# Block-sparse attention with an exact-GELU feed-forward layer: the queries' transposition moved next to the keys', and the scale of 1/8 moved from the queries to the keys

## The chip, the cores and the metric

The kernel runs on one core of one Trainium2 chip. A core has five engines that run on their own and wait for each other by semaphores: TensorE (PE in the profile, with its weight loads as PEld), VectorE (DVE), ScalarE (ACT), GpSimd (POOL) and SyncE (SP). SyncE and GpSimd also issue transfers, each through a queue of its own that is worked off in order. The metric is the device time of one execution in microseconds, as a median of several runs. Before the change it is 324.17 us (three runs, 323.64 to 324.26). One more execution was recorded by the hardware profiler; all times of single instructions come from it.

## What is computed

Four batches, eight heads, 768 tokens, 64 numbers a head. The tokens form 24 blocks of 32. A block of queries sees its neighbours, the first and the last block and three sampled blocks; the first and the last block of queries see everything. The attention's output, 3072 tokens of 512 numbers, goes through a feed-forward layer with GELU:

```python
scores = (1.0 / np.sqrt(D)) * np.matmul(q, k.transpose(0, 1, 3, 2))
mask = np.abs(blk_i - blk_j) <= 1
mask = mask | (blk_i == 0) | (blk_j == 0) | (blk_i == n_blocks - 1) | (blk_j == n_blocks - 1)
# ... and the three sampled key blocks of each query block
attn = softmax(np.where(mask, scores, -1e9))
x = np.matmul(attn, v)            # heads side by side: 3072 x 512
h = x @ w_in                      # 512 -> 2048
out = (0.5 * h * (1.0 + erf(h / np.sqrt(2)))) @ w_out   # 2048 -> 512
```

With D = 64 the scale of the scores is 1/8, a power of two. It may stand on the queries or on the keys: in bf16 both give the same scores.

## The kernel before, in words

The work is cut into nine units. Batch 0 has three (units 0, 1 and 2, of one, two and three groups of 128 tokens), each further batch two halves of three groups. The first half of a batch also holds its dense rounds, those of the first and the last query block (4 rounds); the other rounds take two query blocks each. A second half has six rounds.

The main loop over units `n` (from L574) does this for each: VectorE gathers the sampled keys and values of the next unit into `gb` (L269), FFN1 of unit n runs in eight steps (L451, with GELU on ScalarE in L454), and then comes the attention of unit n + 1, with pieces of FFN2 of unit n between its rounds as filler for PE (L470). In a round (`attention`, L495) PE makes scores of queries `qT` against keys (L305), VectorE takes maxima (L330, or L333 for a dense round), ScalarE takes exponentials (L342), VectorE turns the probabilities (L359; L363 into `ptd` for a dense round), and PE weighs the values (L405, L381). The iteration `it` of that loop issues the scores of round it + 1 and the exponentials of round it; a dictionary of hooks adds work at a chosen `it`, behind the stores that are ready (`store_finished`) and ahead of the filler.

A new batch needs its keys and queries with the head dimension on partitions. For batch 0 PE turns them at the start and ScalarE copies them out (`place_heads`). For the later batches GpSimd loads keys (`kn`) and then queries (`qn`) by token, twelve transfers (L111), during FFN1 of the last unit but one of the batch before. Two transfers on SyncE's queue then turn them:

- `turn_keys` (L117) writes `ptd`. It is hooked in at it = 4 of the second half's attention, while `ptd` is not in use.
- `turn_queries` (L120) writes `qT`, of which there are two buffers by batch. It is issued behind the first step of FFN1 of the second half, where `n` is the last unit of its batch (`fresh`).

At that place VectorE then works off, in order: `place_keys` (L123, from `ptd` into `kv`), a spare key block (L240), the fixed part of the gathers (L253, L258, L260), the 33 sampled gathers (L269) and `scale_queries` (L128), which multiplies all of `qT` by 1/8 in place. In the same step GpSimd starts eight loads of values (`load_v`, L134) for the batch that follows the next one, as long as there is one: so in FFN1 of the second halves of batches 0 and 1, and not in that of batch 2.

SyncE's queue otherwise carries the stores of the output (L461). Their tiles (`os`) have three buffers. In the second half of batch 0 a store falls behind round it = 1; in the second halves of batches 1 and 2 one falls behind it = 0 and one behind it = 3.

Of the kernel before, what the change touches and what calls it, by code (L numbers as in the profile page):

```python
# [19 lines left out]
def kernel(  # L20
# [10 lines left out]
    nc = tc.nc  # L31
    P = 128
    B, H, S, D = q.shape
    assert (B, H, S, D) == (4, 8, 768, 64)
    BL = 32
    NB = S // BL
# [4 lines left out]
    NPR = H // 2  # L41
# [6 lines left out]
    PI = 8  # L48
# [6 lines left out]
    NC = S // P  # L55
# [17 lines left out]
    qT0 = const.tile([P, NC, NPR, P], BF16, name="qT0")  # L73
    qT1 = const.tile([P, (NB + 1) * KC], BF16, name="qT1")
    qTs = [qT0, qT1[:, 0:NPR * S].rearrange("p (c r s) -> p c r s", r=NPR, s=P)]
    k0 = qT1.rearrange("p (n c) -> p n c", c=KC)
# [21 lines left out]
    def keys(b):  # L98
        return kvs[b % 2][:, :, 0:KC]
# [5 lines left out]
    def by_token(x):  # L105
        return x.rearrange("p h c -> p (h c)")[:, 0:S * H * D // P]
# [6 lines left out]

    kTd = ptd.rearrange("p g c x q e -> p (g c x q e)")

    def turn_keys(b):
        nc.sync.dma_start_transpose(out=kTd.rearrange("p (n s) -> p n s", s=P), in_=by_token(kn))  # L117

    def turn_queries(b):
        nc.sync.dma_start_transpose(out=qTs[b % 2].rearrange("p c r s -> p (c r) s"), in_=by_token(qn))  # L120

    def place_keys(b):
        nc.vector.tensor_copy(  # L123
            keys(b)[:, 0:NB].rearrange("p (c n) (r k) -> p c n r k", c=NC, k=BL),
            kTd.rearrange("p (c r n k) -> p c n r k", c=NC, r=NPR, k=BL))

    def scale_queries(b):
        nc.vector.tensor_scalar_mul(qTs[b % 2], qTs[b % 2], 1.0 / 8.0)  # L128

    def load_v(b, h):  # L130
        G, hh = divmod(h, 4)
        c0 = KC + V2 * G + VW * (hh % 2)
        hh ^= G
        nc.gpsimd.dma_start(out=kvs[b % 2][32 * hh:32 * hh + 32, 0:NB, c0:c0 + D],  # L134
                            in_=v[b, h].rearrange("(n p) d -> p n d", p=BL))
# [13 lines left out]
    def hold_loads(m):  # L149

        nc.gpsimd.tensor_copy(mark, g[0:1, m, 0:1])  # L151
# [52 lines left out]
    def block_numbers(js, engine):  # L204
        flat = vf.rearrange("o j r -> o (j r)")
        vals = []
        for c0 in range(js[0] * NR, (js[-1] + 1) * NR, 22):
            c1 = min(c0 + 22, (js[-1] + 1) * NR)
            _, got = nc.values_load_multi_w_load_instructions(
                flat[0:1, c0:c1], engines=[engine], min_val=0, max_val=NB,  # L210
                skip_runtime_bounds_check_because="block numbers are below the number of blocks")
            vals += got if isinstance(got, (tuple, list)) else [got]
        return {j: vals[NR * i:NR * i + NR] for i, j in enumerate(js)}
# [9 lines left out]

    def place_heads(which, pr, pt):
        if which == "k":
            nc.scalar.copy(k0[:, 0:NB, BL * pr:BL * pr + BL].rearrange("q n (a i) -> q n a i", i=PI),
                           pt.rearrange("q i (n a) -> q n a i", n=NB))
        else:
            nc.scalar.mul(qT0[:, :, pr, :].rearrange("q c (p i) -> q c p i", i=PI),
                          pt.rearrange("q i (c p) -> q c p i", c=NC), 1.0 / 8.0)  # L230

    def spaces():

# [8 lines left out]
    def gather_fixed(kT, place):  # L242

        groups = gb.rearrange("p (g x) -> p g x", x=GW)
        js = sorted(place)
        runs = [[j for j in js if place[j] - j == c] for c in sorted({place[j] - j for j in js})]
        for run in runs:
            i0 = place[run[0]]
            assert i0 % 3 == 0
            for lane in range(min(3, len(run))):  # L250
                m, g0 = len(range(lane, len(run), 3)), i0 // 3
                c0, j = BW + KC * lane, run[0] + lane - 1
                nc.vector.tensor_copy(  # L253
                    groups[:, g0:g0 + m, c0:c0 + 3 * BW].rearrange("p g (w c) -> p g w c", c=BW)[:, :, :, 0:KC],
                    kT[:, j:j + 3 * m, :].rearrange("p (g w) c -> p g w c", w=3))
        at = slice(min(place.values()) // 3, max(place.values()) // 3 + 1)
        n = at.stop - at.start
        nc.vector.tensor_copy(groups[:, at, 0:3 * KC].rearrange("p g (l c) -> p g l c", c=KC),  # L258
                              kT[:, None, 0:1, :].to_broadcast([P, n, 3, KC]))
        nc.vector.tensor_copy(  # L260
            groups[:, at, 4 * BW:GW].rearrange("p g (l x) -> p g l x", x=DW)[:, :, :, NR * BW:DW],
            kT[:, None, NB - 1:NB, :].to_broadcast([P, n, 3, KC]))

    def gather(unit, js, at, c0=0, c1=BW, engine=None):

        src = k0 if (unit.b, c1) == (0, KC) else kvs[unit.b % 2][:, :, c0:c1]
        for j in js:
            for r in range(NR):
                (engine or nc.vector).tensor_copy(sampled(unit.place[j], r)[:, None, c0:c1],  # L269
                                                  src[:, bass.ds(at[j][r], 1), :])  # L270
# [175 lines left out]
    def ffn1_step(n, m):  # L446
        T = P * len(units[n].quads)
        hp = psA.tile([P, 2, 512], F32, name="hp", tag="A")
        for i in range(2):
            for ki in range(KIN):  # L450
                nc.tensor.matmul(hp[:, i, 0:T], lhsT=w_in_sb[:, ki, (m + i) * P:(m + i + 1) * P],  # L451
                                 rhs=xTs[n % 2][:, ki, 0:T], start=(ki == 0), stop=(ki == KIN - 1))
        for i in ((0, 2),) if m < KOUT - 2 else ((0, 1), (1, 2)):
            nc.scalar.activation(g[:, m + i[0]:m + i[1], 0:T], hp[:, i[0]:i[1], 0:T], AF.Gelu)  # L454
# [119 lines left out]
    for n, unit in enumerate(units):  # L574
        nxt = units[n + 1] if n + 1 < len(units) else None
        b = unit.b
        fresh = nxt is not None and nxt.b != b
        if nxt is not None and not fresh:
            gather_fixed(k0 if n == 0 else keys(b), nxt.place)
            if n == 0:  # L580
                known |= block_numbers(J0[:3], DVE)
                gather(nxt, J0[:3], known, 0, KC)
                gather(nxt, J0[:3], known, KC, BW)
            elif n == 1:
                known |= block_numbers(J1[:6], DVE)
                gather(nxt, J1[:6], known)
                gather(nxt, J1[6:7], block_numbers(J1[6:7], DVE))
            else:
                gather(nxt, J1[:6], known)
                for js in (J1[6:9], J1[9:11]):  # L590
                    gather(nxt, js, block_numbers(js, DVE))
        for s in range(KOUT // 2):
            ffn1_step(n, 2 * s)
            if s == 0:
                if n == 0:
                    hold_loads(0)
                    for h in range(H):
                        load_v(1, h)
                    nc.gpsimd.tensor_copy(kvs[0][:, :, 0:KC], k0)
                    gather(units[2], J1[7:], block_numbers(J1[7:], POOL), engine=nc.gpsimd)  # L600
                if n > 0 and not fresh and b + 1 < B:
                    hold_loads(0)
                    load_by_token(kn, k, b + 1)
                    load_by_token(qn, q, b + 1)
                if fresh and b + 2 < B:
                    hold_loads(0)
                    for h in range(H):
                        load_v(b + 2, h)
                if fresh:
                    others = block_numbers(J0[7:], DVE)  # L610
            if s == 7 and nxt is not None:
                table(AF.Exp)
            if fresh and s == 0:
                turn_queries(b + 1)
                place_keys(b + 1)
                spare_key(keys(b + 1))
                gather_fixed(keys(b + 1), nxt.place)
                gather(nxt, J0[:7], known)
                gather(nxt, J0[7:], others)
                scale_queries(b + 1)  # L620
        filler = ffn2_pieces(n)
        if nxt is None:
            last_output(n)
        elif n in QUOTAS:
            attention(nxt, filler, *QUOTAS[n],
                      hooks={4: [lambda: turn_keys(1)]} if n == 1 else None)
        elif fresh:
            attention(nxt, filler, [6, 6, 4, 0, 6, 6, 4, 0, 2, 2, 1], (6, 3), late=True)
        else:
            attention(nxt, filler, [8, 8, 5, 5, 6, 2, 2], (3, 6),  # L630
                      hooks={4: [lambda: turn_keys(b + 1)]} if b + 1 < B else None)


# [28 lines left out]
```

## Time and profile before

| what | us |
|---|---|
| median of three runs | 324.17 |
| the profiled execution's own time | 323.12 |
| its span, first to last instruction | 321.3 |
| PE busy in the span | 262.8 |
| VectorE busy | 220.1 |
| ScalarE busy | 208.7 |
| GpSimd busy | 87.1 |
| one turn of queries, issue to landing (least, median, most) | 5.5, 10.0, 11.3 |
| one turn of keys, issue to landing (least, median, most) | 6.1, 6.4, 7.2 |

A row of the order of time begins with start and length in microseconds, then engine, line, operation and tiles, how many instructions are put together, and in square brackets the idle time of the engine just before them and what ended it. "issue" means that the profile shows nothing for which the engine waited. In the groups of instructions "x3 | 2.9, 961" is three instructions, 2.9 us busy, 961 ns each on average. An "SPq" or a transfer in GpSimd's rows is the time that issuing took; the transfer itself lands later.

### The profile page before, as it was taken

To read this page: it belongs to the slowest core of one execution; us is meant where nothing else is said; L and a number is where in the kernel's file an instruction comes from. 1 tells how busy PE (TensorE), PEld (TensorE's weight loads), DVE (VectorE), ACT (ScalarE), POOL (GpSimd) and SP (SyncE) were. 2 spreads that over 40 slices of the span, in tenths; PEclk is the share of its full clock that TensorE was granted. 3 is DMA by queue.
4 is the path that set the end of the run, shared out by engine and by line. 5 is a ranking of instruction groups with operands and counts; after the bars stand their busy time and mean duration, and the time that the engine had idled before them with its cause. 6 is when DMAs were issued, how large, how long until landed. Compare 5 with 4: busy or idle time off the path is not lost.

```text
span 321.3 us, 12117 instructions
## 1 busy us (share of the span) xinstructions
PE 262.8 (82%) x5240; PEld 147.9 (46%) x5240; DVE 220.1 (68%) x544; ACT 208.7 (65%) x374; POOL 87.1 (27%) x147
## 2 busy tenths in 40 slices
PE   1755864985798867999996887999898889989995
PEld 0614722743453444535552444535453555445543
DVE  6488783787497886868694897768588878583000
ACT  9665483489266794688564785688468876777621
POOL 8569766670070000870070000950000000000000
PEclk9999696699999999999997999999999999999999
DMA  7999999797099110596699010993540100011001
GB/s 111 142 115 207 207 121 26 76 146 142 4 155 73 38 37 4 64 148 114 114 147 46 35 37 37 69 162 86 94 93 33 37 4 35 1 37 37 33 35 66
DMA packets 90632, 25.43 MB, mean 79 GB/s; under 512 B 81745, under 2 KB 87634, under 8 KB 90578
## 3 DMA queue, kind: packets, MB, share of 16 engines
q0 software_dynamic: 68352, 13.64, 84.3%
q1 hardware_dynamic: 22226, 11.01, 13.8%
q8 instruction: 41, 0.67, 0.9%
q14 instruction: 13, 0.11, 0.1%
HBM read 27.26 MB, written 6.29 MB: 104 GB/s over the span
## 4 chain that ended last, share of the span: by engine, by line
PE 45%; DVE 16%; DMA 12%; issue 11%; ACT 9%; POOL 5%; DVEq 0%; SPq 0%; ACTq 0%; POOLq 0%
PE hp L451 19%; PE op L470 12%; DMA qT<-qn 7%; ACT pp L342 7%; PE av L405 5%; DVE nm L330 4%; DVE pT L359 4%; PE sc L305 4%; DVE xh L422 3%; DMA w_in_sb<-in_moe_w_in_dram 3%; DMA kv<-in_v_dram 2%; POOL kn L111 2%; PE av L491 2%; POOL qn L111 2%; PE op L491 2%
## 5 line engine op out<-in xcount | busy, mean ns | idle before, releaser
L342 ACT ACTIVATE pp<-sc,nm 128x256 bf16<-128x256 f32 (+1 forms) x192 | 92.2, 592 | 20.3 <-DVE nm L330 9.9
L451 PE MATMUL hp<-xT,w_in_sb 128*128 128x384 bf16 (+2 forms) x576 | 89.3, 320 | 1.8 <-ACT xT L437 1.6
L470 PE MATMUL op<-w_out_sb,g 128*128 128x512 bf16 x336 | 86.9, 385 | 2.7 <-ACT os L459 2.6
L454 ACT ACTIVATE g<-hp 128x768 bf16<-128x768 f32 (+4 forms) x81 | 53.8, 676 | 38.7 <-PE hp L451 38.6
L451 PEld LDWEIGHTS <-w_in_sb 128*128 128x128 bf16 x576 | 57.0, 104 | 35.1 <-issue 4.1
L330 DVE TENSOR_REDUCE nm<-sc 128x4 f32<-128x1024 f32 (+1 forms) x48 | 53.3, 1111 | 8.4 <-PE sc L305 8.1
L269 DVE COPY gb<-kv 128x388 bf16 (+1 forms) x240 | 52.6, 299 | 6.3 <-issue 6.2
L405 PE MATMUL av<-kv,pT 64*32 64x130 bf16 x1760 | 33.9, 223 | 17.9 <-issue 10.3
L470 PEld LDWEIGHTS <-g 128*128 128x128 bf16 x336 | 28.4, 98 | 35.9 <-issue 11.8
L405 PEld LDWEIGHTS <-pT 64*32 64x32 bf16 x2816 | 28.3, 91 | 27.9 <-issue 13.7
L359 DVE STREAM_TRANSPOSE pT<-pp 128x512 f32<-128x512 f32 (+1 forms) x48 | 31.6, 658 | 11.1 <-ACT pp L342 11.1
L151 POOL COPY mark<-g 1x1 bf16<-1x1 bf16 x6 | 4.6, 771 | 113.1 <-ACT g L454 113.1
L437 ACT COPY xT<-tx 128x512 bf16<-128x512 bf16 (+1 forms) x24 | 13.3, 553 | 29.4 <-PE tx L432 29.4
L305 PEld LDWEIGHTS <-qT 64*32 64x32 bf16 x832 | 10.2, 90 | 42.8 <-issue 27.5
L305 PE MATMUL sc<-gb,qT 64*32 64x256 bf16 x704 | 19.6, 280 | 10.8 <-ACT pp L342 10.1
L134 POOL DMA_DIRECT2D kv<-in_v_dram x32 | 23.2, 731 | 5.7 <-DVE pT L359 2.3
L405 PE MATMUL av<-gb,pT 64*32 64x130 bf16 x1056 | 20.9, 225 | 1.4 <-issue 1.3
L369 ACT ACT_TABLE_LOAD x17 | 21.8, 1283 | 0.3
L418 DVE TENSOR_SCALAR den<-av 128x8 f32<-128x8 f32 (+2 forms) x28 | 4.2, 152 | 25.9 <-PE av L405 25.4
L333 DVE TENSOR_REDUCE nm<-sc 128x1 f32<-128x768 f32 x16 | 15.3, 955 | 8.3 <-PE sc L305 8.1
L459 ACT COPY os<-op 128x512 f32<-128x512 f32 (+1 forms) x23 | 13.2, 576 | 9.3 <-PE op L470 5.2
L422 DVE TENSOR_TENSOR xh<-av,rec 128x512 bf16<-128x512 f32 (+2 forms) x28 | 18.3, 652 | 1.0
(63 smaller groups left out, 205.0 us busy)
## 6 DMA issues: line engine op xcount, KB each, us to landing
out_dram<-os SPq DMA_DIRECT2D x23, 256.0 KB, 2.1
kv<-in_v_dram POOLq DMA_DIRECT2D x32, 96.0 KB, 10.3
kn<-in_k_dram POOLq DMA_DIRECT2D x18, 128.0 KB, 4.4
qn<-in_q_dram POOLq DMA_DIRECT2D x18, 128.0 KB, 5.1
w_in_sb<-in_moe_w_in_dram POOLq DMA_DIRECT2D x4, 512.0 KB, 12.4
w_out_sb<-in_moe_w_out_dram POOLq DMA_DIRECT2D x4, 512.0 KB, 17.2
kn<-in_k_dram POOLq DMA_DIRECT2D x2, 384.0 KB, 5.5
qn<-in_q_dram POOLq DMA_DIRECT2D x2, 384.0 KB, 7.1
```

The costliest lines, as they stand in the source:

```text
L134: nc.gpsimd.dma_start(out=kvs[b % 2][32 * hh:32 * hh + 32, 0:NB, c0:c0 + D], in_=v[b, h].rearrange("(n p) d -> p n d", p=BL))
L269: (engine or nc.vector).tensor_copy(sampled(unit.place[j], r)[:, None, c0:c1], src[:, bass.ds(at[j][r], 1), :])
L305: nc.tensor.matmul(o, lhsT=qT[rows, j // 4, pr, BL * (j % 4):BL * (j % 4) + BL], rhs=rhs(rows, pr), start=True, stop=True)
L330: nc.vector.tensor_reduce(out=nm[:, 0:2 * n].rearrange("p (g j) -> p g j", g=2), in_=A4[:, :, 0:n, :], op=ALU.max, axis=AX.X, negate=True)
L342: nc.scalar.activation(dst.rearrange("p (c k e) -> p c e k", e=2, k=BL), src.rearrange("p (c e k) -> p c e k", e=2, k=BL), AF.Exp, bias=bias)
L359: nc.vector.transpose(pt[:, 0:w].bitcast(F32), pp[:, 0:w].bitcast(F32))
L369: nc.scalar.activation(junk, zero[0:1, 0:1], func)
L405: nc.tensor.matmul(av[32 * s:32 * s + 32, h, V2 * G:V2 * G + V2], lhsT=pv[rows, c // 2, :, c % 2], rhs=src[rows], start=(c == 0), stop=(c ...
L422: nc.vector.tensor_tensor(xh[rows, :, 0:m * D].rearrange("p h (x d) -> p h x d", d=D), a[:, :, :, 0:D], rec[rows, :, 0:m, None].to_broadca ...
L451: nc.tensor.matmul(hp[:, i, 0:T], lhsT=w_in_sb[:, ki, (m + i) * P:(m + i + 1) * P], rhs=xTs[n % 2][:, ki, 0:T], start=(ki == 0), stop=(ki ...
L454: nc.scalar.activation(g[:, m + i[0]:m + i[1], 0:T], hp[:, i[0]:i[1], 0:T], AF.Gelu)
L470: nc.tensor.matmul(op, lhsT=g[:, m, t * P:(t + 1) * P], rhs=w_out_sb[:, m, :], start=(m == 0), stop=(m == KOUT - 1))
```

## The change

Both turns are issued by one function, `turn`, keys first, and its hook stands at it = 2 in place of 4. The call of `turn_queries` in FFN1 is gone. `place_keys` is no copy of 3072 elements per partition any more but four multiplications by 1/8, of 768 elements each, one for each pair of heads. `scale_queries` is gone. For batch 0 ScalarE's copy and multiplication change places: the keys are multiplied, the queries copied.

```diff
-    def turn_keys(b):
+    def turn(b):
         nc.sync.dma_start_transpose(out=kTd.rearrange("p (n s) -> p n s", s=P), in_=by_token(kn))
-
-    def turn_queries(b):
         nc.sync.dma_start_transpose(out=qTs[b % 2].rearrange("p c r s -> p (c r) s"), in_=by_token(qn))
 
     def place_keys(b):
-        nc.vector.tensor_copy(
-            keys(b)[:, 0:NB].rearrange("p (c n) (r k) -> p c n r k", c=NC, k=BL),
-            kTd.rearrange("p (c r n k) -> p c n r k", c=NC, r=NPR, k=BL))
-
-    def scale_queries(b):
-        nc.vector.tensor_scalar_mul(qTs[b % 2], qTs[b % 2], 1.0 / 8.0)
+        for pr in range(NPR):
+            nc.vector.tensor_scalar_mul(
+                keys(b)[:, 0:NB, BL * pr:BL * pr + BL].rearrange("p (c n) k -> p c n k", c=NC),
+                kTd.rearrange("p (c r n k) -> p r c n k", c=NC, r=NPR, k=BL)[:, pr], 1.0 / 8.0)
...
         if which == "k":
-            nc.scalar.copy(k0[...], pt...)
-        else:
-            nc.scalar.mul(qT0[...], pt..., 1.0 / 8.0)
+            nc.scalar.mul(k0[...], pt..., 1.0 / 8.0)
+        else:
+            nc.scalar.copy(qT0[...], pt...)
...
             if fresh and s == 0:
-                turn_queries(b + 1)
                 place_keys(b + 1)
...
                 gather(nxt, J0[7:], others)
-                scale_queries(b + 1)
...
-                      hooks={4: [lambda: turn_keys(1)]} if n == 1 else None)
+                      hooks={2: [lambda: turn(1)]} if n == 1 else None)
...
-                      hooks={4: [lambda: turn_keys(b + 1)]} if b + 1 < B else None)
+                      hooks={2: [lambda: turn(b + 1)]} if b + 1 < B else None)
```

More of the change, by code (lines that the diff above doesn't have):

```diff
@@ L225, in place_heads @@
         if which == "k":
-            nc.scalar.copy(k0[:, 0:NB, BL * pr:BL * pr + BL].rearrange("q n (a i) -> q n a i", i=PI),
-                           pt.rearrange("q i (n a) -> q n a i", n=NB))
-        else:
-            nc.scalar.mul(qT0[:, :, pr, :].rearrange("q c (p i) -> q c p i", i=PI),
-                          pt.rearrange("q i (c p) -> q c p i", c=NC), 1.0 / 8.0)
+            nc.scalar.mul(k0[:, 0:NB, BL * pr:BL * pr + BL].rearrange("q n (a i) -> q n a i", i=PI),
+                          pt.rearrange("q i (n a) -> q n a i", n=NB), 1.0 / 8.0)
+        else:
+            nc.scalar.copy(qT0[:, :, pr, :].rearrange("q c (p i) -> q c p i", i=PI),
+                           pt.rearrange("q i (c p) -> q c p i", c=NC))
     def spaces():
```

## The prediction, made before the result was known

> **What bounds the kernel now.** First the page: the span, the granted clock in 40 slices of 8.03 us, the queue that carries instructions, and the chain that ended last.
>
> ```profile
> span 321.3 us, 12117 instructions
> ...
> PEclk9999696699999999999997999999999999999999
> ...
> q8 instruction: 41, 0.67, 0.9%
> ...
> PE 45%; DVE 16%; DMA 12%; issue 11%; ACT 9%; POOL 5%; DVEq 0%; SPq 0%; ACTq 0%; POOLq 0%
> ```
>
> The chain is mostly TensorE. What the change can reach is where PE stands still, so the waits of PE come second (columns: total us, times, longest us):
>
> ```profile
> PE av L405 <- issue: 11.6, 8, 3.1
> ...
> PE sc L305 <- DVE qT L128: 4.6, 2, 3.0
> ```
>
> The second row is what the change can remove: scores that wait for the scaling of the queries. The first is its danger: gaps for which the profile names no releaser. Third, PE in order of time where a batch's first scores follow FFN1:
>
> ```profile
> 87.60 10.56 PE L451 MATMUL hp<-xT,w_in_sb 128*128 128x384 bf16 x64
> 99.74 0.51 PE L305 MATMUL sc<-kv,qT 64*32 64x512 bf16 x8 [1.57 <-DVE qT L128]
> ...
> 157.83 10.56 PE L451 MATMUL hp<-xT,w_in_sb 128*128 128x384 bf16 x64
> 171.43 0.83 PE L305 MATMUL sc<-kv,qT 64*32 64x512 bf16 x8 [3.04 <-DVE qT L128]
> ...
> 174.56 0.51 PE L305 MATMUL sc<-kv,qT 64*32 64x512 bf16 x8
> ...
> 240.58 0.50 PE L305 MATMUL sc<-kv,qT 64*32 64x512 bf16 x8
> ...
> 242.42 0.50 PE L305 MATMUL sc<-kv,qT 64*32 64x512 bf16 x8
> ```
>
> Batch 1 waits 1.57 us and batch 2 waits 3.04 us; batch 3 does not wait. Batch 2 also restarts slowly: from its first to its second scores it takes 174.56 - 171.43 = 3.13 us, batch 3 takes 242.42 - 240.58 = 1.84 us with the same work between; the lone 7 in the page's clock row is this slice (21 x 8.03 = 168.7 us). Fourth, why the queries are late, by the queues of SyncE and of GpSimd and by the time of the queries' turn from issue to landing:
>
> ```profile
> 72.80 3.77 SPq L117 DMA_TRANSPOSE ptd<-kn  x1
> ...
> 88.71 3.77 SPq L120 DMA_TRANSPOSE qT<-qn  x1
> ...
> 143.02 7.12 SPq L461 DMA_DIRECT2D out_dram<-os  x2
> 150.45 4.45 SPq L117 DMA_TRANSPOSE ptd<-kn  x1
> ...
> 221.88 3.86 SPq L117 DMA_TRANSPOSE ptd<-kn  x1
> ```
>
> ```profile
> 64.70 5.28 POOL L111 DMA_DIRECT2D qn<-in_q_dram  x6
> ...
> 90.58 5.96 POOL L134 DMA_DIRECT2D kv<-in_v_dram  x8 [0.26 <-PE hp L451]
> ...
> 137.46 5.26 POOL L111 DMA_DIRECT2D qn<-in_q_dram  x6
> ...
> 160.82 5.86 POOL L134 DMA_DIRECT2D kv<-in_v_dram  x8 [0.37 <-PE hp L451]
> ```
>
> ```profile
> DMA to landing us min/median/max: 5.5/10.0/11.3
> ```
>
> The turn lands after 5.5 us at best and after 10 to 11 us in the two batches where eight loads of values start behind it (90.58 and 160.82). In batch 3 no such loads are left.
>
> **The change part by part.** The profiled execution took 323.12 us, and the sum is made against it; the median of the runs, 324.17 us, stands 1.05 us above.
>
> *The queries' turn leaves FFN1.* The waits of 1.57 and 3.04 us go, and with the second the slow restart, 3.13 - 1.84 = 1.29 us. Together 5.90 us, all on PE's path: in batch 3, without the wait, the scores follow FFN1 directly. FFN1 of batch 1 ends at 87.60 + 10.56 = 98.16, the first scores then at 98.67. Late next are VectorE and ScalarE:
>
> ```profile
> 90.80 7.50 DVE L269 COPY gb<-kv 128x388 bf16 x33
> ...
> 100.29 0.96 DVE L333 TENSOR_REDUCE nm<-sc 128x1 f32<-128x768 f32 x1 [0.61 <-PE sc L305]
> ```
>
> ```profile
> 99.09 1.28 ACT L369 ACT_TABLE_LOAD   x1
> 100.39 0.20 ACT L369 ACTIVATE junk<-zero 1x1 bf16<-1x1 bf16 x1
> ```
>
> VectorE is free of its gathers at 98.30, and ScalarE has its table at 100.59; maxima of 0.96 us from 98.67 on fit between.
>
> *Keys scaled in four pieces, queries' scaling removed.* VectorE's groups with shapes kept apart (busy us, mean ns):
>
> ```profile
> L123 DVE COPY kv<-ptd 128x3072 bf16<-128x3072 bf16 x3 | 2.9, 961 | 0.8 <-issue 0.8
> L128 DVE TENSOR_SCALAR qT<-qT 128x3072 bf16<-128x3072 bf16 x3 | 2.9, 959 | 2.2 <-DMA qT<-qn 2.2
> ...
> L253 DVE COPY gb<-qT 128x768 bf16<-128x768 bf16 x2 | 0.7, 352 | 0.0
> ```
>
> A multiplication over 3072 elements costs what a copy does, so a piece of 768 is priced by the strided copy of 768: 4 x 0.352 = 1.41 us against 0.96, 0.45 us more per batch, ahead of the gathers. These then end at 98.75 and the maxima at 99.71, still 0.88 us before 100.59: ScalarE's table load hides it, and past 0.88 us it would cost one for one. From below a piece cannot beat a quarter of the 959 ns (nothing added); from above I put each piece at the whole copy's 0.96 us, 2.88 us more, which is a rival below. I take 0.45 because L128 and L253 are nearest in operation and in size. The 0.96 us of scaling lies inside the waits counted above; in batch 3 FFN1 covers it, so its removal gains nothing there.
>
> *Batch 0.* ScalarE now multiplies four times for keys and copies four times for queries:
>
> ```profile
> L226 ACT COPY qT<-pk x4: 792/799/804, 7.6 to 11.7; 128x768 bf16<-128x768 bf16 x4
> L229 ACT ACTIVATE qT<-pt x2: 804/810/816, 12.4 to 15.6; 128x768 bf16<-128x768 bf16 x2
> ```
>
> The forms differ by 0.01 us and change places: zero.
>
> *Both turns in the third round.* In the second half of batch 0, where batch 1 is turned, no store lies between the third and the fifth round, so on SyncE the keys' turn stays at 72.80 and the queries' follows at about 76.6. Their load was issued by 69.98 and lands in time by this row of loads (min, median, max):
>
> ```profile
> DMA to landing us min/median/max: 4.4/5.2/11.3
> ```
>
> In the second halves of batches 1 and 2 both turns move ahead of the fourth round's store: in batch 1 the keys' turn to some 143.4, right behind the store at 143.02. The queries' turn needs loads issued until 142.72, landed at about 147.9, and occupies the queue until about 151.7; the second store of the row at 143.02, out by 143.02 + 7.12 = 150.14, waits behind it for some 2 us. Nobody waits for a store here until its buffer comes round, three stores later: zero. The values' loads, now alone, can only finish earlier.
>
> What is not zero is the company of TensorE. PE's gaps without a releaser in the second halves of batches 0, 1 and 2, and the length of those attention stages with a fourth, of batch 3, that has no turn (columns: stretch, length, busy time by engine):
>
> ```profile
> 80.41 0.34 PE L405 MATMUL av<-kv,pT 64*32 64x130 bf16 x17 [2.81 <-issue]
> ...
> 84.41 0.34 PE L405 MATMUL av<-kv,pT 64*32 64x130 bf16 x13 [0.98 <-issue]
> ...
> 154.70 0.24 PE L405 MATMUL av<-gb,pT 64*32 64x130 bf16 x5 [0.60 <-issue]
> ...
> 227.16 0.35 PE L405 MATMUL av<-kv,pT 64*32 64x130 bf16 x15 [1.43 <-issue]
> ```
>
> ```profile
> 137.95:157.83 19.88, 17.93 (x501) 9.43 (x501) 14.02 (x22) 15.48 (x33) 4.77 (x6) 1.00 1.23 126
> 209.26:230.09 20.83, 18.05 (x501) 9.50 (x501) 14.09 (x22) 15.47 (x33) 3.94 (x5) 1.00 1.09 113
> 276.36:296.36 20.00, 18.02 (x502) 9.36 (x501) 13.24 (x21) 15.48 (x33) 0.00 (x0) 1.00 0.08 29
> ```
>
> Every turn in these stages has such a gap within 8 us. I read them as PE's instruction stream held up by the turn's transfer; the trace shows only the nearness. Against the stage without a turn, one turn cost 19.88 - 20.00 = -0.12 and 20.83 - 20.00 = 0.83 us, 0.36 on average: a second turn costs 2 x 0.36 = 0.72 us for those two stages. In batch 0 the second turn starts at 76.6, into the gap of 2.81 us that ends at 80.41 and is paid already; I let it repeat the smaller gap, 0.98 us. From below, the moved keys' turns take their gaps with them: -0.60 - 1.43 = -2.03 us. From above, three turns at 2.81 us, 8.43 us.
>
> Sum: -5.90 + 0.72 + 0.98 = -4.20 us, 318.9 us profiled and 320.0 us as a median.
>
> **The rivals.** *The turns are free of charge.* For it speaks the -0.12 us of batch 1's second half; against it 2.81 us at 80.41. The waits alone go: 324.17 - 5.90 = 318.3 us. The Trainium skill, "Runtime: NRT & Kernel Launch", section "Instruction fetch mechanics", has the sequencer fetch the next block of 256 instructions over its own DMA queue while it executes the current one, and calls the cost mostly hidden; by that rule this rival holds. The trace disagrees in part: its gaps stand in matmul runs that wait for nothing else.
>
> *The second turn starves PE (slower).* Both turns back to back hold up the stream in each second half as the first did in batch 0's, 2.81 + 0.98 = 3.79 us: 3 x 3.79 = 11.37 us, 324.17 - 5.90 + 11.37 = 329.6 us. It decides from 5.90 / 3 = 1.97 us a stage on. Against it: the gaps of 0.60 and 1.43 us in the other two stages. A gap as long as the 3.04 us of batch 2 would bring its slow restart too, another 1.29 us. The Trainium skill, "TensorE: Matmul & The Clock Gate", Part 1, halves the clock after an idle window of about 3.4 us; the trace shows the slow restart already behind 3.04 us of waiting.
>
> *VectorE becomes the bound.* With 2.88 us more for the keys the gathers of batch 1 end at 101.18, past the old start of the maxima (100.29): 0.89 us lost instead of 1.57 gained. In batch 2 at most the slow restart and 0.7 us of the wait remain as gain, in batch 3 some 0.4 us are lost; with 1.70 us for the turns this ends at 324.17 + 0.89 - 1.29 - 0.7 + 0.4 + 1.70 = 325.2 us at worst, and with pieces half as slow near no change.
>
> **How the numbers follow.** The forecast, gain of 5.90 less one to three us for the turns: 0.60. Free turns, or gaps that leave with the moved keys' turn (324.17 - 5.90 - 2.03 = 316.2 us): 0.22. Starved PE: 0.11. VectorE the bound: 0.07. The likeliest time is 320.0 us. Downward the range takes in most of the vanished gaps, 316.7 us; upward a charge of 5.4 us, nearly two of the three at 2.81 us, 323.7 us; outside lie the starved case and the ends. A measurement tells 0.2% (0.65 us) from no change. Faster: 0.60 + 0.22 and a little of the others, 0.84. The same: 0.05. Slower: 0.11.
>
> **What would show it.** The scores of batches 1 and 2 should follow FFN1 at once, and the clock row lose its 7. The keys' pieces should take about 0.35 us each, and the gathers end before the table load does. In the second halves two turns stand back to back; the gaps without releaser should add one to three us there over all three. Wrong is the prediction if those gaps grow beyond 5.90 us, if the first maxima wait for VectorE, or if the queries' load lands later than 147.9 us and drags its turn into FFN1.

## The result and the profile after

The changed kernel takes 319.99 us as a median of 20 runs, the kernel before 323.47 us in 20 runs beside them: a ratio of 0.9884 (95% interval 0.9856 to 0.9912), which is some 3.75 us; the medians lie 3.48 us apart. Two later comparisons gave 321.02 against 322.43 us (0.9843, 0.9774 to 0.9913) and 321.23 against 322.71 us (0.9978, 0.9935 to 1.0020). It is faster by about one per cent; the third comparison by itself cannot be told from no change, and single executions of the changed kernel scatter from 316.80 to 323.80 us. Executions more than 1.5% above the fastest of their kernel count in the medians but not in the ratios; such were the first profiled execution of the changed kernel, of 322.86 us, and those profiled in the rows marked * further down. The profile shown here is of a second execution, of 320.36 us, 2.76 us under the profiled execution of before.

The page: span, granted clock, chain.

```profile
span 318.6 us, 12084 instructions
...
PEclk9998696699599999999999999999999999999999
...
PE 55%; DVE 18%; ACT 10%; issue 8%; DMA 5%; POOL 1%; DVEq 1%; ACTq 0%; POOLq 0%
```

The slice of 168.7 us has its full clock, and DMA's share of the chain fell from 12% to 5%. PE's waits (total us, times, longest us), and PE in order of time behind FFN1 of the second halves of batches 0 and 1:

```profile
PE av L401 <- issue: 14.1, 11, 2.9
PE sc L301 <- ACT pp L338: 12.7, 18, 1.3
```

```profile
88.37 10.56 PE L447 MATMUL hp<-xT,w_in_sb 128*128 128x384 bf16 x64
98.86 0.51 PE L301 MATMUL sc<-kv,qT 64*32 64x512 bf16 x8
...
157.80 10.56 PE L447 MATMUL hp<-xT,w_in_sb 128*128 128x384 bf16 x64
168.29 0.51 PE L301 MATMUL sc<-kv,qT 64*32 64x512 bf16 x8
170.13 0.51 PE L301 MATMUL sc<-kv,qT 64*32 64x512 bf16 x8
```

The scores' wait for the queries is gone; they follow FFN1 at once. What is left of their waits is for ScalarE's exponentials, as before the change. The gaps without a releaser in runs of value matmuls grew from 11.6 to 14.1 us. In the second halves of batches 0, 1 and 2 they are now these:

```profile
80.01 0.34 PE L401 MATMUL av<-kv,pT 64*32 64x130 bf16 x17 [2.81 <-issue]
84.28 0.51 PE L401 MATMUL av<-kv,pT 64*32 64x130 bf16 x13 [0.98 <-issue]
...
150.39 0.30 PE L401 MATMUL av<-gb,pT 64*32 64x130 bf16 x15 [0.95 <-issue]
154.66 0.24 PE L401 MATMUL av<-gb,pT 64*32 64x130 bf16 x6 [1.25 <-issue]
...
219.72 0.50 PE L401 MATMUL av<-kv,pT 64*32 64x130 bf16 x35 [0.97 <-issue]
223.45 0.35 PE L401 MATMUL av<-kv,pT 64*32 64x130 bf16 x16 [0.69 <-issue]
```

Those of batch 0 are as long as before. In batch 1 two gaps stand where one of 0.60 us was, in batch 2 two where one of 1.43 us was. Where time went and came from is seen by stretches. First the dense stages, from the first FFN1 matmul of batch 0's, 1's and 2's second half to that of the next unit, before and after. The columns are start and end, length, the busy time of PE, PEld, DVE, ACT and POOL with their numbers of instructions, the granted clock, and the busy share and GB/s of the transfer engines:

```profile
87.60:127.46 39.86, 32.92 (x694) 17.43 (x694) 32.05 (x76) 26.71 (x48) 6.25 (x9) 1.00 1.30 62
157.83:198.78 40.95, 33.92 (x696) 17.51 (x695) 32.65 (x77) 26.62 (x48) 6.03 (x9) 0.96 1.12 60
230.09:265.87 35.78, 32.70 (x696) 17.29 (x695) 30.00 (x76) 26.40 (x48) 0.00 (x0) 1.00 0.19 47
```

```profile
88.37:125.78 37.41, 32.00 (x689) 17.33 (x694) 31.23 (x76) 26.35 (x48) 6.19 (x9) 1.00 0.98 45
157.80:194.60 36.80, 31.93 (x690) 17.34 (x694) 32.20 (x78) 26.38 (x48) 6.28 (x9) 1.00 0.98 45
226.40:262.07 35.67, 31.60 (x689) 17.23 (x694) 29.33 (x75) 26.36 (x48) 0.00 (x0) 1.00 0.07 25
```

They lost 2.45, 4.15 and 0.11 us, together 6.71. Then the three second halves after the change, from the first scores to the next FFN1:

```profile
65.61:88.37 22.76, 16.07 (x481) 8.74 (x486) 14.23 (x27) 14.65 (x32) 4.47 (x6) 0.85 1.18 130
136.28:157.80 21.52, 17.43 (x496) 9.41 (x501) 14.14 (x25) 15.44 (x33) 4.80 (x6) 1.00 1.31 152
205.09:226.40 21.31, 17.63 (x497) 9.46 (x502) 14.25 (x25) 15.45 (x33) 3.68 (x5) 1.00 1.29 145
```

Against 21.60 us (66.00 to 87.60 before), 19.88 and 20.83 us they grew by 1.16, 1.64 and 0.48, together 3.28 us. Half of the gain went back there. In batch 0's stage the granted clock was 0.85, where it had been 1.00 before. The rest of the difference lies in stages that the change does not touch.

### The profile page after: what moved, and what is told of

Read it like the earlier page. It is cut to its first block, busy times and chain, and to the rows that moved or that the text cites. A ratio compares the mean times of both kernels' runs of the same rounds, so it can differ in the third digit from the quotient of the medians.

```text
span 321.1 us, 12084 instructions
## 1 busy us (share of the span) xinstructions
PE 258.9 (81%) x5197; PEld 149.0 (46%) x5240; DVE 218.6 (68%) x550; ACT 208.0 (65%) x374; POOL 87.2 (27%) x147
## 4 chain that ended last, share of the span: by engine, by line
PE 58%; DVE 15%; ACT 11%; issue 8%; DMA 5%; POOL 1%; DVEq 0%; ACTq 0%; POOLq 0%
PE hp L447 28%; PE op L466 12%; PE av L401 7%; ACT pp L338 7%; DVE nm L326 4%; PE sc L301 4%; DVE pT L355 3%; DMA w_in_sb<-in_moe_w_in_dram 3%; DVE xh L418 3%; DMA kv<-in_v_dram 2%; PE tx L428 2%; PE av L487 2%; PE op L487 2%; DVE nm L329 2%; ACT os L455 1%
## 5 line engine op out<-in xcount | busy, mean ns | idle before, releaser
L466 PE MATMUL op<-w_out_sb,g 128*128 128x512 bf16 x294 | 79.2, 388 | 7.1 <-issue 3.7
L401 PE MATMUL av<-kv,pT 64*32 64x130 bf16 x1760 | 35.3, 229 | 17.9 <-issue 10.6
L401 PEld LDWEIGHTS <-pT 64*32 64x32 bf16 x2816 | 29.4, 94 | 31.2 <-issue 17.5
L301 PEld LDWEIGHTS <-qT 64*32 64x32 bf16 x832 | 10.1, 90 | 38.3 <-issue 27.5
L401 PE MATMUL av<-gb,pT 64*32 64x130 bf16 x1056 | 22.0, 231 | 4.3 <-issue 4.2
```

The costliest lines, as they stand in the source:

```text
L301: nc.tensor.matmul(o, lhsT=qT[rows, j // 4, pr, BL * (j % 4):BL * (j % 4) + BL], rhs=rhs(rows, pr), start=True, stop=True)
L401: nc.tensor.matmul(av[32 * s:32 * s + 32, h, V2 * G:V2 * G + V2], lhsT=pv[rows, c // 2, :, c % 2], rhs=src[rows], start=(c == 0), stop=(c ...
L466: nc.tensor.matmul(op, lhsT=g[:, m, t * P:(t + 1) * P], rhs=w_out_sb[:, m, :], start=(m == 0), stop=(m == KOUT - 1))
```

## The experiments

In the table and the texts here the *second halves*, or stages of batches 0, 1 and 2, are these three stretches. Behind each row stands one profiled execution.

| kernel | median us | before beside it | ratio (95%) | second halves of batches 0, 1, 2 |
|---|---|---|---|---|
| changed | 321.02 | 322.43 | 0.9843 (0.9774 to 0.9913) | 22.76, 21.52, 21.31 |
| no queries' turn * | 318.35 | 322.43 | 0.9811 (0.9742 to 0.9880) | 21.57, 21.29, 20.01 |
| scale alone | 317.55 | 322.43 | 0.9867 (0.9820 to 0.9913) | 21.52, 19.84, 20.22 |
| scale, values later | 316.81 | 322.43 | 0.9843 (0.9789 to 0.9898) | 21.60, 19.83, 19.96 |
| both turns at it = 4 | 320.18 | 322.87 | 0.9848 (0.9778 to 0.9918) | 23.75, 20.20, 20.25 |
| scale, keys' turn at it = 2 * | 320.01 | 322.87 | 0.9928 (0.9880 to 0.9975) | 22.61, 21.28, 20.50 |
| second transfer a plain copy | 318.31 | 322.87 | 0.9894 (0.9857 to 0.9931) | 21.58, 21.23, 20.52 |
| values later alone | 316.86 | 322.87 | 0.9883 (0.9834 to 0.9932) | 20.84, 20.22, 20.28 |
| both transfers plain copies | 315.03 | 323.07 | 0.9761 (0.9703 to 0.9818) | 20.15, 20.48, 19.97 |
| batch 1 loaded and turned early * | 326.24 | 323.07 | 1.0071 (1.0034 to 1.0108) | 21.24, 20.41, 20.23 |
| scale, values later, once more * | 318.39 | 322.71 | 0.9804 (0.9741 to 0.9867) | 21.26, 20.05, 20.30 |
| changed, once more | 321.23 | 322.71 | 0.9978 (0.9935 to 1.0020) | 22.67, 21.75, 20.78 |

The medians are of 4 to 12 runs and differ by up to 1.6 us between two comparisons of the same kernel, and medians and ratios do not always put two kernels in the same order. The stretches carry the argument, where they repeat: batch 1's took 19.83 to 20.41 us in all six profiles with the keys' turn at it = 4 and the queries' in FFN1. The second half of batch 3, which no kernel here changes, took 20.00 to 21.27 us, so a difference below one microsecond in a single stretch shows little.

**The changed kernel again.**

> The changed kernel as it is, for a profile and a time beside the others of this call. Theory A (the waits of 1.57 and 3.04 us and the slow restart of 1.29 us are gone, and each second turn holds up PE's instruction stream in its second half by 1 to 2 us): about 3.5 us under the kernel before; no wait of the first dense scores for the queries in any batch; the attention stages of the three second halves longer than before by 1 to 2 us each. Theory B (the second turn is free, and the long second halves of the first profile are chance): the second halves at 20 to 21 us again and the gain nearer to 5.9 us.

The profile above: no wait for the queries, and second halves 0.5 to 1.6 us longer, where 1 to 2 us were expected. The time came out 1.41 us under that of before by the medians and some 5 us by the ratio, where 3.5 us were expected.

**Without the queries' turn.** The transfer is left out:

```diff
     def turn(b):
         nc.sync.dma_start_transpose(out=kTd..., in_=by_token(kn))
-        nc.sync.dma_start_transpose(out=qTs[b % 2]..., in_=by_token(qn))
```

> The changed kernel without the queries' turn: the queries of batches 1 to 3 are not turned at all (old ones are used), so the transfer is left out of the work. Theory A: the second halves lose what the second turn costs, 1 to 2 us each, and the whole is 3 to 5 us faster than the changed kernel, some 6 to 8 us faster than before. Theory B: within 0.5 us of the changed kernel.

2.67 us less than the changed kernel by the medians of the same comparison, less than theory A asked for and more than theory B. The stages tell more: those of batches 0 and 2 lost 1.2 and 1.3 us, that of batch 1 kept its length and its gaps (PE in order of time):

```profile
151.93 0.30 PE L400 MATMUL av<-gb,pT 64*32 64x130 bf16 x14 [1.27 <-issue]
...
155.66 0.24 PE L400 MATMUL av<-gb,pT 64*32 64x130 bf16 x5 [0.70 <-issue]
```

So in batch 1 it is not the second turn that costs most. What else moved is the keys' turn, from it = 4 to it = 2; this is called theory A2 below.

**The scale alone.** Turns as before:

```diff
-            nc.vector.tensor_copy(keys(b)..., kTd...)
+        for pr in range(NPR):
+            nc.vector.tensor_scalar_mul(keys(b)..., kTd..., 1.0 / 8.0)
...
-                scale_queries(b + 1)
```

> Only the scale moves to the keys; the turns stay where they were before (keys at it = 4, queries in FFN1). If the scaling of 0.96 us lies on the path behind the queries' landing, the wait of batch 1 falls from 1.57 to some 0.6 us and that of batch 2 from 3.04 to some 2.1 us, and with a wait that short the slow restart of 1.29 us may go as well: 1.9 to 3.2 us faster than before. If the pieces cost VectorE much more than 0.45 us a batch, the first maxima wait for it and less than 1 us is gained.

The wait of batch 1 came out at 0.62 us, as expected. In batch 2 the scores start 0.94 us behind FFN1, not 2.1, and at full clock; the turn landed after 10.2 us here and after 11.3 us before. The row names ScalarE, but the turn, issued at 156.08 us, landed at 166.28, as the scores began:

```profile
96.51 0.50 PE L303 MATMUL sc<-kv,qT 64*32 64x512 bf16 x8 [0.62 <-DMA qT<-qn]
...
154.78 10.56 PE L449 MATMUL hp<-xT,w_in_sb 128*128 128x384 bf16 x64
166.28 0.51 PE L303 MATMUL sc<-kv,qT 64*32 64x512 bf16 x8 [0.94 <-ACT g L452]
```

That is 0.95 + 2.10 + 1.29 = 4.34 us less than before, beyond the expected 3.2, with second halves as before; the ratio gives some 4.3 us. By the median this kernel is 3.47 us under the changed one, but their ratios to the kernel before, 0.9867 and 0.9843, do not tell the two apart.

**The scale, and the values' loads later.** The turns stay as before; GpSimd issues the loads behind the fifth step of FFN1:

```diff
-                if fresh and b + 2 < B:
-                    hold_loads(0)
-                    for h in range(H):
-                        load_v(b + 2, h)
...
+            if s == 4 and fresh and b + 2 < B:
+                hold_loads(8)
+                for h in range(H):
+                    load_v(b + 2, h)
```

> The scale on the keys, the queries' turn in FFN1 as before, but the eight loads of values issued behind the fifth step of FFN1 instead of the first. Theory A: without those loads the turn lands after 5.5 us in all batches, no dense scores wait, and no second turn stands in a second half: 5 to 6 us faster than before, 1.5 to 2.5 us faster than the changed kernel. Rival: the turn lands late for another reason, the waits stay at 0.6 and 2.1 us, and the time is that of the kernel with the scale alone. Second rival: the values' loads now lie beside the dense rounds and lengthen these by more than 1 us.

The queries' turn from issue to landing (min, median, max), and the first dense scores of batch 1:

```profile
DMA to landing us min/median/max: 5.6/5.6/7.2
```

```profile
86.22 10.56 PE L449 MATMUL hp<-xT,w_in_sb 128*128 128x384 bf16 x64
96.71 0.51 PE L303 MATMUL sc<-kv,qT 64*32 64x512 bf16 x8
```

No wait, no second turn in a second half, and a median 4.21 us under that of the changed kernel in the same comparison, though with the same ratio of 0.9843. The dense stages, beside which the loads now lie, took 38.23, 36.74 and 35.68 us: the first 0.8 us more than in the profile above, as in one other profile of the changed kernel (38.42), the others the same.

**Both turns at it = 4.**

```diff
-                      hooks={2: [lambda: turn(b + 1)]} if b + 1 < B else None)
+                      hooks={4: [lambda: turn(b + 1)]} if b + 1 < B else None)
```

(and the same for batch 1's turn in unit 2.)

> The changed kernel with both turns at it = 4 instead of 2. Theory A2 (formed after the first four runs: what lengthens the second halves of batches 1 and 2 is mostly that the keys' turn now begins at it = 2 and holds up the block of PE's instructions that the first run of value matmuls needs; without any queries' turn that gap stayed): the gaps before the first runs of value matmuls in these two stages go, the stages return to 20 to 21 us, and the kernel is 1.5 to 3 us faster than the changed one. Theory A (the second turn as such costs): the stages stay at 21.5 to 23 us and the time within 1 us of the changed kernel.

The stages of batches 1 and 2 fell to 20.20 and 20.25 us, as A2 has it, although two turns stand in each. That of batch 0, where the hook changes no place in the queue, took 23.75 us with a gap of 3.76 us, and the time as a whole moved by less than a microsecond, not by the 1.5 to 3 us expected: theory A2 holds for two stages and says nothing of the first.

**The scale, and the keys' turn alone at it = 2.**

```diff
-                      hooks={4: [lambda: turn_keys(b + 1)]} if b + 1 < B else None)
+                      hooks={2: [lambda: turn_keys(b + 1)]} if b + 1 < B else None)
```

(and the same for batch 1's turn in unit 2.)

> Scale on the keys, the queries' turn in FFN1 as before, and the keys' turn alone moved to it = 2. Theory A2: the second halves of batches 1 and 2 show the gaps of the changed kernel at the first value matmuls, and are 1 to 1.5 us longer than with the keys' turn at it = 4: 1.5 to 3 us slower than the kernel with the scale alone. Theory A: no second turn, no cost, the same time as the kernel with the scale alone.

2.46 us above the kernel with the scale alone by the medians of two comparisons, and batch 1's stage 1.44 us longer (21.28 against 19.84) without any second turn: A2. That of batch 2 grew by 0.28 us alone (20.50 against 20.22), where 1 to 1.5 us were expected. The transfers by queue (packets, MB, share of 16 engines) from 6.72 to 11.62 us behind that stage's first scores, with the keys' turn at it = 2, and then the same stretch with the turn at it = 4:

```profile
q1 hardware_dynamic: 2861, 0.96, 103.0%
q0 software_dynamic: 1172, 0.15, 47.1%
...
ptd<-kn SPq DMA_TRANSPOSE x1, 8.4
```

```profile
q0 software_dynamic: 986, 0.12, 39.7%
q1 hardware_dynamic: 144, 0.26, 14.3%
q8 instruction: 1, 0.02, 1.4%
```

The queue q8 brings instructions, and q1 holds the turn. In the first stretch, 146.90 to 151.80 us, no packet of instructions moves; the turn's packets run from 147.93 to 152.36 us, and the next block of instructions starts at 152.12. In the second stretch one block of 16 KB comes in, starting at 145.03, before the turn.

These blocks are what the gaps hang on. In all profiles, every gap over 0.4 us in the value matmuls of the three second halves for which no releaser is named ends 1.2 to 1.6 us behind the end of a block. In batch 1's stage the block ahead of the first of these matmuls starts 9.9 to 10.1 us behind the first scores in the kernels with the keys' turn at it = 4, and 11.7 to 12.0 us behind them in those with it at it = 2.

Batch 0's stage fits neither theory. There the keys' turn has the same place in the queue whatever the hook, and with that turn alone the stage took 22.61 us here, as long as with both in the changed kernel. The granted clock in it was 0.85, as in the changed kernel; with the scale alone it was 0.92 and the stage took 21.52 us. What the second turn costs in this stage apart from the clock is not shown.

The turn at it = 2 also meets the last loads of the queries (1172 packets of GpSimd's queue) and lands after 8.4 us.

**The second transfer a plain copy.**

```diff
-        nc.sync.dma_start_transpose(out=qTs[b % 2]..., in_=by_token(qn))
+        nc.sync.dma_start(out=qTs[b % 2]..., in_=by_token(qn))
```

> The changed kernel with the second transfer a plain copy of the same bytes from the same tile to the same tile, so the queries of batches 1 to 3 are not turned. If it is the transposing that holds up PE's instructions, the gaps shrink to those of the kernel without a second turn (the second halves of batch 0 and 2 about 1 us shorter than in the changed kernel). If it is any transfer of that size, the gaps stay as in the changed kernel.

21.58, 21.23 and 20.52 us: batch 0's stage as without a second transfer, that of batch 2 0.8 us under the changed kernel's in the profile above and 0.3 us under it in the later one. By this run the transposing transfer costs what a copy of the same bytes doesn't, but in no stage by more than the clock or the scatter could do; the run with two plain copies below is the firmer one.

**The values' loads later alone.** The edit above made in the kernel before, with VectorE still scaling the queries.

> The kernel before with one edit: the eight loads of values issued behind the fifth step of FFN1 instead of the first; the queries are still scaled by VectorE. If the values' loads make the turn of the queries late, it lands after some 5.5 us in all batches, VectorE scales right behind its gathers, and the waits of 1.57 and 3.04 us fall to 1 us or less: 3 to 5 us faster than before. If something else delays the turn, waits and time stay.

The turn landed after 5.5 to 7.2 us, the scores followed FFN1 directly in both batches, and the median is 6.01 us under that of before, more than expected; the ratio gives some 3.8 us, as expected. The loads of values were what made the queries late.

**Both transfers plain copies.**

```diff
-        nc.sync.dma_start_transpose(out=kTd..., in_=by_token(kn))
+        nc.sync.dma_start(out=kTd, in_=by_token(kn))
```

(and the queries' likewise.)

> The changed kernel with both transfers plain copies of the same bytes at the same place, so neither keys nor queries of batches 1 to 3 are turned. If the transposing transfers hold up PE's instructions, the gap of 2.8 to 3.1 us in the second half of batch 0 and the gaps at the first value matmuls of batches 1 and 2 go or fall to half, and the three stages take about 19.5, 20 and 20 us instead of 22.96, 21.78 and 21.56. If the gaps belong to the instruction stream alone, or to any transfer of this size, the stages stay within 0.5 us of the changed kernel's.

The gap of batch 0's stage fell to half of 2.81 us, and the three stages to 20.15, 20.48 and 19.97 us, 4.99 us less than in the changed kernel's profile above and 4.60 us less than in its later one:

```profile
76.51 0.34 PE L401 MATMUL av<-kv,pT 64*32 64x130 bf16 x17 [1.36 <-issue]
80.51 0.34 PE L401 MATMUL av<-kv,pT 64*32 64x130 bf16 x13 [0.99 <-issue]
```

In batch 1's stage the block ahead of the first value matmuls starts 9.9 us behind the first scores again, with the transfers at it = 2. So the transposing holds up PE's instructions, by 4.6 to 5.0 us over the three stages against plain copies. Which trait of it does so (its length, its small packets, its place on the transfer engines) these runs do not tell apart; the copies landed after 3.5 to 6.6 us, the two turns of the changed kernel after 7.0 to 8.5 us. Half of the gap of batch 0 stays with copies.

**Batch 1 loaded and turned early.** The kernel with the scale and the values' loads later, and in it:

```diff
                     for h in range(H):
                         load_v(1, h)
+                    load_by_token(kn, k, 1)
+                    load_by_token(qn, q, 1)
...
+                if n == 1:
+                    turn_keys(1)
+                    turn_queries(1)
```

(and without batch 1's turns and loads at their old places.)

> The kernel with the scale on the keys and the values' loads later (queries turned in FFN1, keys at it = 4), and in it keys and queries of batch 1 loaded one unit earlier and both turned in FFN1 of the unit before the second half of batch 0. If a turn costs nothing beside FFN1, where PE takes few instructions, and the gap of 2.9 us in that second half comes from the turn, the stage falls from 21.8 to about 19.5 us and the kernel is some 2 us faster than the one it is built from. If the gap is not the turn's, the stage stays at 21.8 us. Against it works GpSimd, which issues twelve loads more before it gathers for that stage: if its gathers end too late, the stage starts later instead.

Slower. What stood against it came about (PE, then GpSimd):

```profile
57.14 0.48 PE L403 MATMUL av<-kv,pT 64*32 64x130 bf16 x17 [5.76 <-issue]
...
76.68 0.92 PE L303 MATMUL sc<-gb,qT 64*32 64x256 bf16 x16 [8.11 <-DVE gb L267]
```

```profile
66.62 6.49 POOL L267 COPY gb<-kv 128x388 bf16 x12 [1.04 <-issue]
```

GpSimd's gathers for the stage end at 73.11 us behind twelve more loads, where they ended at 53.43 us in the kernel that this one is built from. VectorE stands still for 10.21 us, waiting for the first of them, and PE loses 8.11 us there and 5.76 us in the stage before. The stage itself took 21.24 us with a slow restart in it and no gap over 0.71 us. That fits the reading that its gap belongs to the turn, but the run doesn't price it.

**The best kernel and the changed one once more.**

> The kernel with the scale on the keys, the queries' turn in FFN1 and the values' loads later, once more beside the changed kernel. If its lead is real, its median is 3 us or more under the changed kernel's, as in the first call (316.81 against 321.02 us), and the stages show why: the three second halves 1 to 1.5 us shorter each, the dense stages equal.

> The changed kernel once more, beside the one with the values' loads later: about 320 us, second halves of about 23, 21.8 and 21.6 us or more, and no wait of the dense scores for the queries.

2.84 us apart, a little under the 3 expected; second halves of 21.26, 20.05 and 20.30 against 22.67, 21.75 and 20.78 us, the third only 0.48 us shorter. With the scale on the keys and the values' loads later, all runs together have a median of 317.55 us (12 runs), the changed kernel one of 320.37 us (38 runs). By these medians it beats both kernels, and by its median of 316.86 us so does the edit of the loads alone. By the ratios it leads the changed kernel in this comparison (0.9804 against 0.9978) and not in the first (0.9843 both).

## Why the prediction was right

*The queries' turn leaves FFN1 (-5.90).* Right. The dense stages lost 6.71 us in the profile shown and 4.79 in the profile of the last run. Batch 2's stage took 36.80 us in the first of these, where 40.95 less the wait and the restart is 36.62. The cause given for the late turn, the loads of values behind it, holds by two experiments, one that moved only those loads and one that moved those and the scale.

*Keys in four pieces (nothing, with 0.88 us of cover).* Right. The pieces took 356 ns where 352 were forecast, but the next began before the last one ended, so that four cost 1.17 us and not 1.41:

```profile
L122 DVE TENSOR_SCALAR kv<-ptd 128x768 bf16<-128x768 bf16 x12 | 3.5, 356 | 0.8 <-issue 0.8
```

```profile
87.51 1.17 DVE L122 TENSOR_SCALAR kv<-ptd 128x768 bf16<-128x768 bf16 x4 [0.27 <-issue]
91.61 7.52 DVE L265 COPY gb<-kv 128x388 bf16 x33
99.42 0.96 DVE L329 TENSOR_REDUCE nm<-sc 128x1 f32<-128x768 f32 x1 [0.29 <-PE sc L301]
```

The maxima wait for the scores and not for VectorE.

*Both turns in the third round (places in the queue).* Right: 76.6 and 147.9 us were forecast for the queries' turns, and they were issued at 76.87 and 147.03.

```profile
72.41 4.22 SPq L117 DMA_TRANSPOSE ptd<-kn  x1
76.87 4.11 SPq L118 DMA_TRANSPOSE qT<-qn  x1
142.03 4.79 SPq L117 DMA_TRANSPOSE ptd<-kn  x1
147.03 4.37 SPq L118 DMA_TRANSPOSE qT<-qn  x1
```

*The company of TensorE (+0.72 and +0.98).* The mechanism was right, the term too small and in part put down to the wrong turn. The second halves grew by 3.28 us here and by 2.89 us in the last run's profile, not by 1.70. The step that failed is "a second turn costs 2 x 0.36 = 0.72 us for those two stages": it left the keys' turn at the price that it had at it = 4. In batch 1's stage the keys' turn at it = 2 costs 1.4 us by itself (21.28 against 19.84), and the second turn only 0.2 to 0.5 us more (21.52 and 21.75). The price of 0.36 us was taken against one execution of the stage without a turn, 20.00 us; over all profiles that stage took up to 21.27 us, so the price lay within the scatter.

The lower bound, that the moved turns take their gaps with them, did not come about: 0.60 us of gaps became 2.20 in batch 1, and 1.43 became 1.66 in batch 2. In batch 0's stage the forecast of 0.98 us stands beside 1.16, but not by the way forecast. A second gap of that kind did not come; the two gaps, 2.81 and 0.98 us in the profile shown, are as long as before. What came on top is the clock, at half speed behind the gap and 0.85 over the stage against 1.00 before. That the size fits is luck.

The forecast of -4.20 us stands beside some -3.75 by the ratio and -3.48 by the medians. That 320.0 us was met to a hundredth is chance: the kernel before had a median of 323.47 us in the longer comparison, not 324.17, and that made up for the term that was too small.

The first rival, by which turns are free, falls: the second halves grew by 3.28 us. The rule of the Trainium skill, "Runtime: NRT & Kernel Launch", section "Instruction fetch mechanics", that the cost of crossing into the next block is mostly hidden, falls with it in the stages with a turn, where PE stood still for 0.69 to 2.81 us behind late blocks. The second rival, starved PE, was the right mechanism at little more than half the price at which it decides: 3.28 / 3 = 1.1 us a stage against 1.97. VectorE never became the bound.

## What to carry to other kernels

A wait for a transfer has two cures: start it earlier, or take away what runs beside it. Before starting it earlier, look at what it will run beside, engines' instructions among it; here the cheaper cure was to start other loads four steps later. When several small edits come as one, run each alone: the scale alone and the loads alone each gave about as much as the whole (ratios of 0.9867 and 0.9883 against 0.9843 to 0.9978), and one part, the move of the keys' turn, cost 1.4 us in one stage.

## What the runs showed of the hardware that had not been expected

A transposing transfer of 0.8 MB can put off PE's next block of instructions. No block came in over the stretch of 4.9 us shown above, and PE stood still in runs of small matmuls, which use up 256 matmuls and weight loads in 1.3 us (128 of each from 74.03 to 75.32 us in the kernel before). Beside FFN1, with 128 of them in 10.56 us, the same transfer cost nothing: FFN1 took 10.56 us with it and without it. A turn does not shut the blocks out altogether. In the kernel before, the packets of batch 1's keys' turn ran from 151.66 to 156.09 us, and a block came in from 152.46 to 153.41. When a block is asked for, these traces do not show.

The granted clock fell to half in or just behind gaps shorter than three microseconds, and not always. In the kernel with the values' loads later alone (PE in order of time, and the stretch of its second row with its clock, 0.50):

```profile
118.06 0.30 PE L405 MATMUL av<-kv,pT 64*32 64x130 bf16 x4 [2.23 <-issue]
118.69 2.77 PE L470 MATMUL op<-w_out_sb,g 128*128 128x512 bf16 x6 [0.33 <-issue]
```

```profile
118.69:121.46 2.77, 2.77 (x14) 0.83 (x21) 1.43 (x3) 0.00 (x0) 0.00 (x0) 0.50 0.03 6
```

Six output matmuls took 2.77 us behind a gap of 2.23 us, where 1.47 is usual; in the kernel before, a gap of 2.81 us at 80.41 was followed by none of this. Clock losses of that kind seem to be a part of the scatter between executions of one kernel: of the changed kernel's 20, the one of 316.80 us had a mean granted clock of 0.989 and the one of 322.86 us one of 0.956, though the order by clock is not the order by time throughout.
